# Relative-position bias factors built by matmuls from a sliding one-hot constant instead of through a DRAM buffer, in a fused attention and MLP kernel

## The chip, the cores and the metric

One core of one Trainium2 chip runs the whole program. The metric is device time in microseconds (us) of one execution, the median over several timed runs.

## The reference

Attention with a bucketed relative-position bias, then a two-layer MLP with a sine gate. B = 8 sequences, H = 8 heads, S = 576 positions, D = 64.

```python
scores = scale * np.matmul(q, k.transpose(0, 1, 3, 2))      # [8, 8, 576, 576]
rel = pos[:, None] - pos[None, :]
bucket = ...                                                # of |rel|: 0..31, 31 from |rel| near 128 on
scores = scores + bias_table[bucket].transpose(2, 0, 1)[None]
attn = softmax(scores)
x = np.matmul(attn, v)  ->  [4608, 512]
h = x @ w_in                                                # [4608, 2048]
s = np.sin(alpha * h)
g = h + s * s / (alpha + 1e-09)
out = g @ w_out                                             # [4608, 512]
```

The bias depends on a head and on the distance alone, and every distance from about 128 on shares bucket 31. So exp(score + bias) is exp(score) times a factor in a band around the diagonal, once the last bucket's value is subtracted; outside the band the factor is 1.

## The kernel before

**Tiling.** Scores are computed transposed (128 keys on the partitions, 512 queries along the row) for two heads at a time (a "pair", p = 0 to 3). A unit of kind "A" is one block of 128 keys for a pair: two matmuls of 64 rows, then one exp on ACT of 128x1024 (`ex` in `plan_unit`, L723), then on DVE the multiplication of the columns near the diagonal by the band factors (`bd`, L754). Kind "C" is the 64 keys left over, for which a pair shares one block-diagonal key tile `kts`; its band multiplication is on POOL or DVE (L740, factors `mhr`). "B" and "X" are the 64 queries left over. `plan_av` then multiplies with the values `vs`/`vhs` on PE, `norm_av` divides by the row sums on DVE (L967, L968), and for batch t = 0 PE transposes the result and ACT or DVE copies it into `xT` (L560, L562).

**Batches.** The loop over t = 0 to 7 does one sequence's attention, then a block of 512 tokens of the MLP: `plan_moe_in` (h on PE, sine on ACT at L1083, square on ACT at L1090 or DVE at L1092, g on DVE at L1097) and `plan_mo` (g times w_out on PE). The matmuls of `plan_mo` fill the next batch's attention on PE. The exps and the sines use two activation tables, so ACT loads a table twice per batch (L1161). All exps of a batch come before its first sine.

**What sets the order.** Every instruction belongs to a `Task` with an estimated cost per engine, dependencies, a priority and an earliest time (`nb`). `Plan.run` walks a modelled clock and issues tasks, which fixes the order on each engine; the engines then run in that order and wait where data is missing. `HEAD_PRI` overrides the priorities of numbered tasks. Where PE would stand idle early on, the planner inserts matmuls of zeros (`zz`) into a free bank.

**The head.** For t = 0, q and k are loaded in natural layout: pair 0 into `natx` by SP and ACT, pairs 1 to 3 into `nat1` by POOL; PE transposes them (L573, L579; `plan_tr`), DVE copies them to `kT`/`qT` (L562), POOL copies the block-diagonal `kt` (L602). For t = 1 they are loaded into `nat2` by POOL and transposed likewise; from t = 2 on they go through DRAM buffers `staged_k`/`staged_q` and DMA transposes. The values of t = 0 are loaded in float32 into the space of `w_out16` and cast by POOL (L441, L444). w_in, `nat2`, w_out and the values of t = 1 follow on POOL's queue.

**The band factors.** `plan_table` multiplies the table `tabN` by a constant that subtracts the last row (`less_last`), takes the exp on ACT (`tabE`), and multiplies by a one-hot constant `phi_sb` (32x512), which gives one row of 512 distances for each head. ACT copies the row to `e_sb` (L625), a DMA writes it five times to a DRAM buffer `e_dram`, and five DMAs on SP's queue read it back with a stride of one element per partition, which slides the row along the partitions: three into `m2r` (heads 0-1, 2-3, 4-7), two into `mhr`. The factors lie reversed there and are read backwards (`m2 = m2r[:, :, ::-1]`).

```python
load_m2r(nc.sync, 0, 2, 0)
load_mhr(nc.sync)
load_m2r(nc.sync, 2, 4, 3)
load_m2r(nc.sync, 4, H, 4)
for h in range(2, H):
    load_v32(h)
```

Of the kernel before, what the change touches and what calls it, by code (L numbers as in the profile page):

```python
# [34 lines left out]
LAT = {"PE": 0.2, "ACT": 0.18, "DVE": 0.18, "POOL": 0.2, "SP": 2.4}  # L35
NBUF = {"ut": 2, "u": 2, "g": 2, "s16": 3, "sq": 3, "outs": 5, "xn": 6}
PAIRS = ((0, 1), (2, 3), (4, 5))
BANKS = {"h": (0, 1, 2, 3, 4, 5), "av": (6, 7), "mo": (7, 6)}

# [21 lines left out]
class Plan:  # L61
# [86 lines left out]
    def run(self, t0):  # L148
        free = dict(t0)
        todo = list(self.tasks)  # L150
        while todo:
# [21 lines left out]
            for e, c in cands.items():  # L173
                if not c:
                    continue
                s0 = min(x[0] for x in c)
                st, t = min(((x[0], x[1]) for x in c if x[0] <= s0 + SLACK[e]),
                            key=lambda x: (x[1].pri, x[0]))
                fin = st + t.engs[e]
                if best is None or (st, fin) < best[:2]:  # L180
                    best = (st, fin, e, t)
# [32 lines left out]
T_START = {"PE": 4.25, "ACT": 5.2, "DVE": 5.05, "POOL": 5.5, "SP": 5.0}  # L214
SPLIT = {0: 3, 1: 3}
PRI_S = 0
T_WI = 16.4
T_TAB = 4.9
T_PHI = 5.4
T_CL = 9.6  # L220
T_FIRST = (4.3, 5.35)
T_PAIR = ((7.05, 8.1), (8.9, 10.6), (12.5, 13.4))
PRI_TR = (350, 950, 1250)
T_VT = 9.7
T_ACT = ()
T_M2 = (12.4, 14.6, 16.0, 16.0)
T_MH = 13.5
T_RST = 20.0
T_WL = 25.0
T_V0 = (6.5, 8.8, 16.4, 16.9, 17.4, 17.9, 18.4, 18.9)  # L230
T_P3 = 8.3
# [5 lines left out]
T_LD = 33.0  # L237
# [4 lines left out]
SQ = {"ACT": 0.52, "DVE": 0.38}  # L242
T_V = ((15.0, 15.0), (53.5, 53.5))
T_TR1 = (35.5, 39.0)
T_W = (24.2, 27.0, 33.0, 33.0)
T_WO = (42.0, 45.0, 47.8, 51.0)
WARM0 = 7
WARM1 = 0
# [18 lines left out]
}  # L267
SIN_SET = "trig_and_small"
SLACK = {"PE": 0.02, "ACT": 0.02, "DVE": 0.02, "POOL": 0.02, "SP": 0.02}
# [14 lines left out]
def kernel(  # L284
# [26 lines left out]
    NE = 5  # L311
# [14 lines left out]
    last_np = np.eye(NB, dtype=np.float32)  # L326
    last_np[NB - 1] -= 1.0
    phi_h = nc.inline_tensor(phi_np, "phi_const")
    last_h = nc.inline_tensor(last_np, "last_const")
# [8 lines left out]
    m2r = sgl.tile([128, H, XW], F16, name="m2r")  # L338
    mhr = sgl.tile([128, NP, 192], F16, name="mhr")
    m2 = m2r[:, :, ::-1]  # L340
    mh = mhr[:, :, ::-1]
# [13 lines left out]
    tabE = sgl.tile([NB, H], F16, name="tabE")  # L355
    phi_sb = sgl.tile([NB, EW], F16, name="phi_sb")
    less_last = sgl.tile([NB, NB], F32, name="less_last")
    e_sb = sgl.tile([H, EW], F16, name="e_sb")
    alphaN = sgl.tile([NF, 128], F32, name="alphaN")
    idf_sb = sgl.tile([NF, NF], F32, name="idf_sb")  # L360
# [43 lines left out]

    def stage_kq(t):
        for dst, src in ((staged_k, k), (staged_q, q)):
            nc.gpsimd.dma_start(
                out=dst.ap()[t].rearrange("s (h d) -> s h d", h=H),
                in_=src[t].rearrange("h s d -> s h d"),
            )  # L410

    def load_kqT(t):
        nc.sync.dma_start_transpose(out=kTs[t % 2][:, :, :], in_=staged_k.ap()[t])
        nc.sync.dma_start_transpose(out=qTs[t % 2][:, :, :], in_=staged_q.ap()[t])

    def load_kt(t):
        for z in range(2):
            r = slice(64 * z, 64 * z + 64)
            nc.gpsimd.tensor_copy(out=kts[t % 2][r, :, r], in_=kTs[t % 2][r, :, 512:S])  # L419

    def load_v16(t):
        vp = v[t].rearrange("h s d -> s h d")
        for c in range(4):
            nc.gpsimd.dma_start(  # L424
                out=vs[t % 2][:, c, :, 0:D], in_=vp[128 * c : 128 * c + 128],
            )
# [3 lines left out]
    def load_v32(h):  # L430
        nc.sync.dma_start(out=vst[:, h], in_=v[0, h, 0:512].rearrange("(c p) d -> p c d", p=128))
# [29 lines left out]
    def load_w_out16():  # L461
        src = moe_w_out.rearrange("(f p) n -> p f n", p=128)
        for fh in range(4):
            nc.gpsimd.dma_start(
# [782 lines left out]
```

## Time and profile before

| | |
|---|---|
| timed runs | 373.47, 374.05, 375.78 us, median 374.05 us |
| span of the profiled execution, first to last instruction | 372.5 us |
| the profiled execution's own time | the page gives its span alone; the timed runs lie 1.0 to 3.3 us above it, their median 1.55 us |
| PE busy | 363.7 us (98% of the span) |
| ACT busy | 318.3 us (85%) |
| DVE busy | 258.8 us (69%) |
| POOL busy | 89.2 us (24%) |
| the chain that ended last | 87% on PE; the rest, almost all of it, in its first 52.4 us |

The page names engines PE (matmul), PEld (weight load), DVE, ACT, POOL and SP; a q behind a name is the engine's queue of DMA issues. A row of the timeline gives the start, the duration, the engine, the line, the operation and its tiles, and in brackets how long the engine stood idle before it and for whom. A row by windows gives the length of the window, then the busy time of PE, PEld, DVE, ACT and POOL, then PE's granted clock (1.00 is full), the DMA engines' share and their rate. A busy PE is modelled, and matmuls overlap, so PE's rows read a little too full.

### The profile page before, as it was taken

The page shows a single profiled execution, that of the slowest core. Times are in us where ns is not written, and L with a number is a line of the kernel's source. Part 1 is how long each engine was busy: PE and PEld are TensorE (multiplying, and loading weights), DVE is VectorE, ACT ScalarE, POOL GpSimd, SP SyncE. Part 2 cuts the span into 40 slices and gives each one's busy share as a digit, 9 for nine tenths or more (in the row PEclk, how much of TensorE's full clock was granted, in tenths as well). Part 3 has the DMA queues.
Part 4 walks back from the last instruction along what each step waited for, and adds up shares of the span by engine and source line. Part 5 has one row for each costly group of instructions (what it writes and reads, how often), then busy time and mean ns, then how long its engine had stood idle before and what let it go on. Part 6 is the DMA issues. An engine that isn't in the chain of part 4 may idle for free.

```text
span 372.5 us, 8907 instructions
## 1 busy us (share of the span) xinstructions
PE 363.7 (98%) x3563; PEld 195.3 (52%) x3563; DVE 258.8 (69%) x555; ACT 318.3 (85%) x436; POOL 89.2 (24%) x130
## 2 busy tenths in 40 slices
PE   6989989999999999999999999999999999999996
PEld 2455445644465445784554456444676455444443
DVE  4697966678776967597659866787669675879100
ACT  2898999989998999799989999899979997999211
POOL 5575360065000730064003700090006000000000
PEclk9599999999999999999999999999999999999999
DMA  9799999299824996199917992699249121000122
GB/s 167 152 191 208 203 170 155 61 146 123 113 60 99 115 151 112 48 161 138 135 48 135 126 169 59 115 114 171 60 111 118 65 58 48 7 18 13 59 85 84
DMA packets 149690, 40.69 MB, mean 109 GB/s; under 512 B 137144, under 2 KB 144656, under 8 KB 149648
## 3 DMA queue, kind: packets, MB, share of 16 engines
q0 software_dynamic: 94928, 17.47, 58.1%
q1 hardware_dynamic: 54352, 22.30, 25.5%
q8 instruction: 28, 0.46, 0.5%
q10 hardware_dynamic: 368, 0.34, 0.3%
q14 instruction: 14, 0.11, 0.1%
HBM read 37.73 MB, written 16.56 MB: 146 GB/s over the span
## 4 chain that ended last, share of the span: by engine, by line
PE 87%; DVE 4%; DMA 3%; ACT 3%; issue 1%; SPq 0%; ACTq 0%; DVEq 0%
PE pb L478 86%; DVE g L1097 1%; DMA tabN<-in_bias_table_dram 1%; DVE u L754 1%; DMA m2r<-e_dram 1%; DMA e_dram<-e_sb 1%; ACT sq L1090 1%; PE pb L1039 1%; ACT s L1083 1%; ACT nat L723 1%; DVE sq L1092 0%; DVE kT L562 0%; ACT L1161 0%; SPq L501 0%; DVE xn L968 0%
## 5 line engine op out<-in xcount | busy, mean ns | idle before, releaser
L723 ACT ACTIVATE u<-pb 128x1024 f16<-128x1024 f32 (+1 forms) x146 | 137.6, 1015 | 8.8 <-PE pb L478 7.4
L478 PE MATMUL pb<-w_out,g 128*128 128x512 f16 (+2 forms) x592 | 138.7, 374 | 0.5 <-DVE kT L562 0.5
L478 PE MATMUL pb<-xT,w_in 128*128 128x512 f16 (+4 forms) x704 | 127.5, 340 | 0.0
L1097 DVE SCALAR_TENSOR_TENSOR g<-sq,inv_a,pb 128x512 f16<-128x512 f16 x144 | 101.1, 743 | 7.7 <-ACT sq L1090 3.8
L1083 ACT ACTIVATE s<-pb,alphaT 128x512 f16<-128x512 f32 x144 | 92.9, 692 | 11.1 <-PE pb L478 10.2
L478 PEld LDWEIGHTS <-w_in 128*128 128x128 f16 x704 | 64.6, 98 | 57.1
L754 DVE TENSOR_TENSOR u<-u,m2r 128x768 f16<-128x768 f16 (+1 forms) x128 | 63.2, 498 | 35.6 <-ACT u L723 33.7
L478 PEld LDWEIGHTS <-g 128*128 128x128 f16 x592 | 54.0, 98 | 60.3 <-issue 5.4
L478 PEld LDWEIGHTS <-u 128*128 128x128 f16 x1152 | 43.1, 97 | 10.9 <-issue 5.8
L1090 ACT ACTIVATE sq<-s 128x512 f16<-128x512 f16 x75 | 46.8, 637 | 1.2 <-DVE g L1097 0.3
L419 POOL COPY kt<-kT 64x256 f16<-64x256 f16 x12 | 5.1, 428 | 174.2 <-DMA kT<-staged_k 144.9
L478 PE MATMUL pb<-qT,kT 64*128 64x64 f16 (+1 forms) x512 | 44.0, 293 | 1.6 <-ACT u L723 0.6
L478 PE MATMUL pb<-v,u 128*128 128x65 f16 x1024 | 43.7, 193 | 0.0
L1092 DVE TENSOR_TENSOR sq<-s 128x512 f16<-128x512 f16 x69 | 28.8, 427 | 12.1 <-ACT s L1083 11.2
L968 DVE TENSOR_TENSOR xn<-pb,rd 128x256 f16<-128x256 f32 (+2 forms) x59 | 28.5, 483 | 2.0
L478 PEld LDWEIGHTS <-kT 64*128 64x128 f16 x512 | 16.3, 95 | 23.1 <-issue 16.2
L478 PE MATMUL pb<-vh,u 128*128 128x130 f16 x128 | 28.3, 221 | 0.0
L424 POOL DMA_DIRECT2D v<-in_v_dram x28 | 24.8, 898 | 6.9 <-DMA w_in<-in_moe_w_in_dram 2.6
L560 ACT ACTIVATE outs<-pb 128x512 f32<-128x512 f32 (+2 forms) x10 | 5.5, 554 | 19.9 <-PE pb L478 19.9
L562 DVE COPY outs<-pb 128x512 f32<-128x512 f32 x27 | 18.5, 686 | 3.8 <-PE pb L478 3.8
L1161 ACT ACT_TABLE_LOAD x15 | 19.2, 1283 | 0.3
L967 DVE RECIPROCAL rd<-pb 128x4 f32<-128x4 f32 (+2 forms) x59 | 11.0, 186 | 10.8 <-PE pb L478 10.7
(74 smaller groups left out, 181.2 us busy)
## 6 DMA issues: line engine op xcount, KB each, us to landing
out_dram<-outs SPq DMA_DIRECT2D x35, 256.0 KB, 2.3
v<-in_v_dram POOLq DMA_DIRECT2D x28, 128.0 KB, 5.1
staged_k<-in_k_dram POOLq DMA_DIRECT2D x6, 576.0 KB, 9.6
staged_q<-in_q_dram POOLq DMA_DIRECT2D x6, 576.0 KB, 12.0
w_out<-in_moe_w_out_dram POOLq DMA_DIRECT2D x4, 512.0 KB, 17.4
w_out<-in_v_dram SPq DMA_DIRECT2D x8, 128.0 KB, 5.2
w_in<-in_moe_w_in_dram POOLq DMA_DIRECT2D x2, 512.0 KB, 6.3
w_in<-in_moe_w_in_dram POOLq DMA_DIRECT2D x1, 1024.0 KB, 11.6
```

The source lines that it names most:

```text
L424: nc.gpsimd.dma_start(out=vs[t % 2][:, c, :, 0:D], in_=vp[128 * c : 128 * c + 128],)
L478: nc.tensor.matmul(out=out, lhsT=lhsT, rhs=rhs, start=start, stop=stop)
L562: k_of(e).tensor_copy(out=o, in_=i)
L723: nc.scalar.activation(out=o, in_=x, func=AF.Exp, scale=0.125)
L754: nc.vector.tensor_tensor(out=io, in0=io, in1=m2[:, 2 * p : 2 * p + 2, x0 : x0 + hi - lo], op=ALU.mult)
L967: nc.vector.reciprocal(out=r, in_=x[:, :, :, D])
L968: nc.vector.tensor_tensor(out=xn[:, 0:n].rearrange("p c (z d) -> p c z d", z=2), in0=x[:, :, :, 0:D], in1=r.unsqueeze(3).to_broadcast([128 ...
L1083: nc.scalar.activation(out=s16.v, in_=h.v, func=AF.Sin, scale=alphaT[:, f : f + 1])
L1090: nc.scalar.activation(out=sq.v, in_=s16.v, func=AF.Square)
L1092: k_of(e).tensor_tensor(out=sq.v, in0=s16.v, in1=s16.v, op=ALU.mult)
L1097: nc.vector.scalar_tensor_tensor(out=gcell[b].v[:, f, :], in0=sq.v, scalar=inv_a[:, f : f + 1], in1=h.v, op0=ALU.mult, op1=ALU.add,)
L1161: nc.scalar.preload_act_table_set(name)
```

## The change

- **Band factors on PE.** The one-hot constant becomes 128x512: four copies of the 32 buckets, each shifted by one distance, and in its last four columns a mark for each copy. The table's exp now has 128 rows (four copies); DVE multiplies it by the marks into `tab4` (128 rows, 8 heads x 4). A matmul with 128 neighbouring columns of the constant as weights and `tab4` as the moving operand (32 columns) gives four columns of the band for all heads at once, already slid along the partitions. 96 such matmuls, in three groups of 32, make a 128x8x384 band in three PSUM pairs; ACT copies two of them into `m2` and DVE the third (1024 float32 columns each). `mh` is copied from `m2`, one half by DVE and one by POOL. The DRAM buffer, its write and the five reads, and `e_sb`, are gone; the factors are read forwards.
- **Table first.** `tabN` is loaded as the first DMA on POOL's queue; it was the fourth on ACT's. `less_last` is made on DVE from the identity instead of loaded. The constant (now 128 KB, it was 32 KB) is the third DMA on ACT's queue; it was the third on SP's.
- **First values by chunks of keys.** Four loads of 256 KB each for 128 keys of all heads, all issued at the start on SP's queue; before, eight of 128 KB, one for each head, two at the start and six behind the band reads. The eight casts on POOL, one for each head, now need all four.
- **Order.** The third pair load follows the second at once on POOL. w_in is issued on POOL right behind them, before any value is cast. w_out, the values of t = 1 and the staging of t = 2 follow as transfers with their own modelled queue. Most earliest times are replaced by dependencies on modelled transfers, the remaining ones have new numbers, and `HEAD_PRI` lists a priority for every early task.

ACT from the cast of the first q on (natx: the first pair; pb: PSUM; the tile that `order` prints as m is `m2`; `u` rows are exps). Before:

```order
L540 ACTIVATE natx<-natx 96x6x64
L616 ACTIVATE tabE<-pb 32x8
L625 ACTIVATE e_sb<-pb 8x512
L626 DMA e_dram<-e_sb 8x5x512
L723 ACTIVATE u<-pb 128x2x512 x3
L723 ACTIVATE u<-pb 128x512
L723 ACTIVATE u<-pb 128x2x512 x2
```

Now:

```order
L561 ACTIVATE natx<-natx 96x6x64
L633 ACTIVATE tabE<-pb 128x8
L577 ACTIVATE m_76<-pb 128x8x128
L795 ACTIVATE u<-pb 128x2x512 x3
L795 ACTIVATE u<-pb 128x512
L577 ACTIVATE m_76<-pb 128x8x128
L795 ACTIVATE u<-pb 128x2x512 x5
```

One copy of a third of the band stands ahead of the first exp and another behind the fourth; the copy of `e_sb` and the DMA issue are gone.

DVE from the copy of alpha on to the first multiplications by the band (CAST of m is the copy of the band's last third out of PSUM). Before:

```order
L665 COPY alphaT<-pb 128x16
L666 TENSOR_SCALAR tmp_a<-alphaT 128x16
L669 RECIPROCAL inv_a<-tmp_a 128x16
L562 COPY qT_68<-pb 128x576
L754 TENSOR_TENSOR u<-u,m2r 128x2x384
L754 TENSOR_TENSOR u<-u,m2r 128x2x256
L562 COPY kT_66<-pb 128x576
```

Now:

```order
L734 COPY alphaT<-pb 128x16
L737 TENSOR_SCALAR tmp_a<-alphaT 128x16
L740 RECIPROCAL inv_a<-tmp_a 128x16
L579 COPY qT_68<-pb 128x576
L666 COPY mh<-m_76 64x768
L579 CAST m_76<-pb 128x8x128
L579 COPY kT_66<-pb 128x576
L827 TENSOR_TENSOR u<-u,m_76 128x2x256
L827 TENSOR_TENSOR u<-u,m_76 128x2x384 x2
```

Two copies, one half of `mh` and a third of the band, now stand between the copy of pair 2's q and the first multiplication, and pair 3's k is copied before it too. Further up, the product `tab4` now stands between the first copies of k and q.

POOL behind the first pair loads (nat is `nat1`, kt the block-diagonal keys, v and vh the values). Before:

```order
L531 CAST idf_sb<-id_sb 16x16
L602 COPY kt_70<-kT_66 64x64 x2
L454 DMA nat_96<-in_k_dram 96x2x384
L454 DMA nat_96<-in_q_dram 96x2x384
L602 COPY kt_70<-kT_66 64x64 x2
L441 CAST vh_74<-w_out_79 64x4x64 x2
L602 COPY kt_70<-kT_66 64x64 x2
L444 CAST v_72<-w_out_79 128x4x64 x2
```

Now:

```order
L487 DMA nat_96<-in_k_dram 96x2x384
L487 DMA nat_96<-in_q_dram 96x2x384
L619 COPY kt_70<-kT_66 64x64 x2
L492 DMA w_in_78<-in_moe_w_in_dram 128x4x512 x2
L492 DMA w_in_78<-in_moe_w_in_dram 128x4x1024
L619 COPY kt_70<-kT_66 64x64 x2
```

The last pair load now precedes the first copy to `kt`, and the loads of w_in follow that copy; before, they stood among the casts of values. Behind these rows come memsets, two casts of values, the `kt` copy of pair 2, a third cast and one half of `mh`, the other six casts of values later. The table's load and the identity's cast stand ahead of all pair loads.

On PE the first group of 32 band matmuls stands ahead of the first scores; then come two A units, both transposes of pair 1, an A and a C unit, the first transpose of pair 2, the second group, an A unit, the second transpose of pair 2, and the third group. Before, the scores followed the 32x512 product at once, and one transpose stood behind each of the first three units.

The diff, cut to its core:

```diff
+LAT = {..., "DMA": 1.9}
-T_WI = 16.4
+T_WI = 8.0
-T_FIRST = (4.3, 5.35)
+T_FIRST = (4.75, 5.65)
-T_V0 = (6.5, 8.8, 16.4, 16.9, 17.4, 17.9, 18.4, 18.9)
+T_V0 = (12.3,) * 8
 HEAD_PRI = {
-    0: 3652.1, 1: 2400.7, 3: 2400.3, ...
+    0: 9015.789063, 1: 9014.578049, 2: 9014.559597, ...
...
-    e_dram = nc.dram_tensor("e_dram", [NE, 4 * H, EW], F16, kind="Internal")
-    phi_np = np.zeros((NB, EW), dtype=np.float16)
-    for x in range(EW - 1):
-        phi_np[bt[abs(x - 255)], x] = 1.0
+    phi_np = np.zeros((NJ * NB, EW), dtype=np.float16)          # NJ = 4
+    for j in range(NJ):
+        for x in range(EW - NJ):
+            phi_np[NB * j + bt[abs(x - 252 - j)], x] = 1.0
+        phi_np[NB * j : NB * j + NB, EW - NJ + j] = 1.0
...
+    P_.dma_start(out=tabN, in_=bias_table)
...
-    nc.scalar.dma_start(out=less_last, in_=last_h.ap())
-    nc.scalar.dma_start(out=tabN, in_=bias_table)
-    nc.sync.dma_start(out=phi_sb, in_=phi_h.ap())
+    nc.scalar.dma_start(out=phi_sb, in_=phi_h.ap())
...
-    load_v32(0)
-    load_v32(1)
+    for c in range(4):
+        load_v32(c)
...
+    load_pair(3)
...
+    nc.vector.tensor_scalar(out=less_last, in0=idf_sb..., scalar1=idf_sb[:, NB - 1 : NB], op0=ALU.subtract)
...
+        def spread(e):
+            nc.vector.tensor_tensor(
+                out=tab4, in0=tabE.unsqueeze(2).to_broadcast([NJ * NB, H, NJ]),
+                in1=phi_sb[:, EW - NJ : EW].unsqueeze(1).to_broadcast([NJ * NB, H, NJ]), op=ALU.mult,
+            )
...
+        for k, w in enumerate((1, 2, 0)):
+            def mm(e, b=b, w=w, s=0):
+                o = bank(b, 2).rearrange("p k x -> p (k x)")
+                for i in range(n // NJ // 2 * s, n // NJ // 2 * (s + 1)):
+                    x0 = EW - NJ - 128 - n * w - NJ * i
+                    full(o[:, NJ * H * i : NJ * H * (i + 1)], phi_sb[:, x0 : x0 + 128],
+                         tab4.rearrange("p h j -> p (h j)"), True, True)
+            def cp(e, b=b, w=w):
+                copy_on(e, m2[:, :, n * w : n * (w + 1)]..., bank(b, 2)...)
+        for z in range(2):
+            def half(e, z=z):
+                k_of(e).tensor_copy(out=mh[r], in_=m2[r, z::2, 64 * z : 64 * z + 192])
...
-        for h in range(2, H):
-            load_v32(h)
...
-        x = plan.add({"POOL": 1.7}, lambda e: load_nat2(), [], 9021, nb=T_RST, after=[x])
-        x = plan.add({"POOL": 3.2}, lambda e: load_w_out16(), [], 9022, nb=T_WL, after=[x] + vdone)
+    def plan_loads():
+        ...                        # w_in, nat2, w_out, values of t = 1, staging of t = 2,
+        ...                        # each a POOL issue and a transfer on a modelled DMA queue
```

More of the change, by code (lines that the diff above doesn't have):

```diff
@@ L34 @@
 D_TAIL = 0.72
-LAT = {"PE": 0.2, "ACT": 0.18, "DVE": 0.18, "POOL": 0.2, "SP": 2.4}
+LAT = {"PE": 0.2, "ACT": 0.18, "DVE": 0.18, "POOL": 0.2, "SP": 2.4, "DMA": 1.9}
 NBUF = {"ut": 2, "u": 2, "g": 2, "s16": 3, "sq": 3, "outs": 5, "xn": 6}
@@ L241 @@
 NORM0 = 1200
[L242 to L246, printed above, removed]
+SQ = {"ACT": 0.53, "DVE": 0.41}
 WARM0 = 7
+COLD = (99.0, 99.0, 1.0)
 WARM1 = 0
@@ L310 @@
     EW = 512
-    NE = 5
+    NJ = 4
     ctx.enter_context(tc.manual_schedule())
@@ L512 @@
     )
+    P_.tensor_copy(out=idf_sb, in_=id_sb[0:NB, 0:NB])
     for kq, src in ((0, k), (1, q)):
@@ L608, in plan_table @@
     def plan_table():
-        a, b = Buf("h"), Buf("h")
+        a = Buf("h")
         def less(e):
-            full(bank(a)[0:NB, 0:H], less_last, tabN, True, True)
+            full(bank(a)[:, 0:H], less_last.rearrange("a j b -> a (j b)"), tabN, True, True)
         def ex(e):
-            nc.scalar.activation(out=tabE, in_=bank(a)[0:NB, 0:H], func=AF.Exp)
-        x = plan.add({"PE": 0.15}, less, [], -1200, nb=T_TAB, new=[a])
-        x = plan.add({"ACT": 0.15}, ex, [x], -1200, use=[a])
-        def mm(e):
-            full(bank(b)[0:H, 0:EW], tabE, phi_sb, True, True)
@@ L742, in bd @@
                 )
-            d = plan.add({"POOL": 0.6} if t == 0 and p else {"DVE": 0.25 if two else 0.15}, bd, [x],
-                         base + 10, nb=late, use=[ub])
+            d = plan.add({"POOL": 0.6} if t == 0 and p else {"DVE": 0.25 if two else 0.15}, bd, [x] + band,
+                         base + 10, use=[ub])
             for pp in (p, p + 1) if two else (p,):
```

256 lines of the change are left out of this document (151 added, 105 removed), and 39 rows, old and new, of the table HEAD_PRI.

## The prediction

> **What bounds the kernel now.** I read the page's totals first, then the busy time by windows, then the chain of waits, then the groups of single windows.
>
> ```profile
> PE 363.7 (98%) x3563; PEld 195.3 (52%) x3563; DVE 258.8 (69%) x555; ACT 318.3 (85%) x436; POOL 89.2 (24%) x130
> ...
> 4.82:8.23 3.41, 1.47 (x22) 1.01 (x21) 1.34 (x3) 0.73 (x3) 1.66 (x4) 1.00 1.19 173
> 8.23:11.65 3.42, 3.42 (x38) 1.68 (x38) 1.65 (x3) 2.60 (x3) 0.71 (x3) 0.50 1.13 189
> 11.65:15.06 3.41, 3.41 (x35) 1.58 (x33) 2.05 (x6) 3.21 (x4) 2.30 (x8) 0.50 0.35 71
> 15.06:18.46 3.40, 3.40 (x35) 1.52 (x33) 2.89 (x6) 2.88 (x5) 1.93 (x9) 0.50 0.92 214
> 18.46:29.67 11.21, 10.02 (x177) 6.95 (x176) 10.95 (x30) 10.59 (x16) 8.74 (x16) 1.00 1.16 197
> 29.67:52.40 22.73, 21.40 (x220) 10.39 (x217) 17.26 (x32) 21.67 (x36) 11.35 (x19) 1.00 1.39 199
> 52.40:369.70 317.30, 317.20 (x3046) 171.11 (x3045) 220.66 (x471) 275.07 (x373) 58.66 (x65) 1.00 0.80 97
> ```
>
> From 52.40 to 369.70 PE stands idle for 0.10 us (317.30 - 317.20). The change adds and removes nothing there, so those 317 us stay. Whatever it does must show before 52.4 us: as an earlier start of PE's unbroken work (29.67, the first matmul with w_in) or as less PE idle between 29.67 and 52.40, which is 22.73 - 21.40 = 1.33 us.
>
> ```profile
> 2.22 4.77 DMA tabN<-in_bias_table_dram
> ...
> 8.19 0.59 ACT e_sb L625
> 8.81 3.42 DMA e_dram<-e_sb
> ...
> 13.96 4.43 DMA m2r<-e_dram
> 18.48 1.61 DVE u L754 x3
> ```
>
> The chain runs through the DRAM bounce: from the table's load at 2.22 to the first multiplication by the last heads' factors at 18.48. Read alone, it promises ten microseconds. But a chain names only the wait that ended last. Beside it stands ACT:
>
> ```profile
> 9.39 2.18 ACT L723 ACTIVATE u<-pb 128x1024 f16<-128x1024 f32 x2 [0.61 <-PE pb L478]
> ...
> 26.30 2.43 ACT L723 ACTIVATE u<-pb 128x1024 f16<-128x1024 f32 x3 [0.59 <-PE pb L478]
> ...
> L723 ACT ACTIVATE u<-pb 128x1024 f16<-128x1024 f32 x16 | 15.8, 1026 | 1.5 <-PE pb L478 1.4
> L723 ACT ACTIVATE u<-pb 128x512 f16<-128x512 f32 x4 | 2.4, 600 | 0.6 <-PE pb L478 0.5
> ```
>
> The 20 exps of t = 0 run from 9.39 to 28.73 (26.30 + 2.43), 19.34 us, and do not need the factors at all. The idle before them is 1.5 + 0.6 = 2.1, of which 0.61 lies before 9.39; so 1.5 us of the 19.34 are gaps and 17.85 are work. No sine may come before the last exp. DVE is the second wall: 10.95 of the 11.21 us from 18.46 on are busy, because its multiplications began late.
>
> **The change, part by part.** *When the first exp starts.*
>
> ```profile
> 7.12 0.20 PE L478 MATMUL pb<-tabN,less_last 32*32 32x8 f32 x2 [1.94 <-DMA tabN<-in_bias_table_dram]
> ...
> 5.04 0.52 ACT L540 ACTIVATE natx<-natx 96x384 f16<-96x384 f32 x1 [1.07 <-DMA natx<-in_q_dram]
> 5.17 0.76 DVE L562 COPY kT<-pb 128x576 f16<-128x576 f16 x1
> ...
> 8.74 0.61 PE L478 MATMUL pb<-qT,kT 64*128 64x512 f16 x2
> ```
>
> PE stood 1.94 us for the table, and the transposes of q stood behind it. As the first DMA on POOL the table's issue moves from 2.22 to 0.81. I take its landing as before 5.5, since a landing at 0.81 + 4.77 = 5.58 is the same duration without the queue ahead of it. ACT's cast of q ends at 5.56, so the table's exp ends near 5.9. DVE's copy of k ends at 5.93; the product `tab4` follows when the constant has landed. It stands behind the first q on ACT's queue, which landed at 5.04; with four times the bytes I take 6.3. Then `tab4` is there at 6.5, the first band group runs from 6.7 to 7.6, the first scores until 7.85 and ACT's first band copy until 8.7 to 9.0. The first exp starts at 9.0, against 9.39: -0.4 us, although the table is 2 us earlier.
>
> *The 96 band matmuls.* No row shows 32 columns on 128 weight columns. The nearest:
>
> ```profile
> 48.43 0.64 PE L478 MATMUL pb<-qT,kT 64*128 64x64 f16 x32
> 41.95 0.45 PE L579 MATMUL pb<-id_sb,nat 96*64 96x96 f16 x12
> 19.18 0.41 PE L478 MATMUL pb<-v,u 128*128 128x65 f16 x8
> ...
> 9.28 0.69 PE L579 MATMUL pb<-id_sb,nat 96*64 96x96 f16 x12
> ```
>
> Per instruction these rows give 20, 38 and 51 ns at full clock, so a group of 32 lies between 0.64 and 1.6 us; part of each row is the pipeline's fill, which a group pays once, and I take 0.9. At the half clock the third row becomes the fourth (0.45 to 0.69 us), so I take up to 2.1 there. Groups two and three hide behind exps that are already queued, if PE is at full clock.
>
> *Copies out of PSUM.*
>
> ```profile
> 52.50 6.70 ACT L723 ACTIVATE u<-pb 128x1024 f16<-128x1024 f32 x7
> ```
>
> One 128x1024 exp takes 1.03 us in its row and 0.95 from start to start ((6.70 - 1.03) / 6 in this run of seven), and a band copy on ACT has the same size: two of them. The first precedes the first exp and is in the 9.0; the second adds **0.95**. ACT's 0.59 for `e_sb` fell before 9.39 and frees nothing later. DVE's third copy is priced by a line through two rows of the profile:
>
> ```profile
> L562 DVE COPY outs<-pb 128x512 f32<-128x512 f32 x27 | 18.5, 686 | 3.8 <-PE pb L478 3.8
> ...
> L562 DVE COPY kT<-pb 128x576 f16<-128x576 f16 x6 | 4.5, 756 | 2.2 <-PE pb L579 2.1
> ...
> L754 DVE TENSOR_TENSOR u<-u,m2r 128x768 f16<-128x768 f16 x8 | 4.3, 552 | 0.0
> ...
> L754 DVE TENSOR_TENSOR u<-u,m2r 128x512 f16<-128x512 f16 x8 | 4.5, 568 | 0.2 <-DMA m2r<-e_dram 0.2
> ```
>
> The first of these is the page's, the second the first 60 us's, the last two those of 15.4 to 30.8. Per column the first two give 1.3 ns, so 1024 columns cost 1.1 to 1.4 us; with 0.4 for a half of `mh`, DVE has 1.6 us more ahead of its first multiplication. Its idle time before 18.46 covers that (3.41 - 2.05 and 3.42 - 1.65 in two windows). The multiplications start near 15.5 to 16, as they do now, but none of the later ones waits for a DMA, and the 256-column form, 568 ns on average, has stalls in it that no busy engine explains (the larger form takes 552). I let DVE end up to 1.2 us earlier than now; ACT then decides.
>
> *Sum for t = 0.* First exp 9.0, work 17.85, second copy 0.95, gaps 0.4 instead of 1.5: last exp at 28.2, against 28.73. That is 0.5 earlier; with DVE's earlier end on the tail behind it I take **-0.6** for PE's unbroken start.
>
> *The MLP block of t = 0 and the start of t = 1.* The order gives ACT 8 squares and 3 copies of t = 1's keys and queries before the next exps, where it now has 10 and 4:
>
> ```profile
> L1090 ACT ACTIVATE sq<-s 128x512 f16<-128x512 f16 x10 | 6.6, 657 | 0.0
> L560 ACT ACTIVATE kT<-pb 128x576 f16<-128x576 f16 x2 | 1.4, 682 | 0.0
> L560 ACT ACTIVATE qT<-pb 128x576 f16<-128x576 f16 x2 | 1.3, 672 | 0.0
> ```
>
> That is 2 x 0.66 + 0.68 = 2.0 us less on ACT, which was full there (21.67 of 22.73), and 3 transposes instead of 0 come behind the first matmuls of `plan_mo`. DVE gets the two squares and stays near 16 us. So PE waits less for ACT and DVE; it can win at most its 1.33 us of idle, and I take **-1.0**. The earlier w_in, `nat2` and w_out gain nothing: no wait of PE before 52.4 is for them.
>
> *Total:* -0.6 - 1.0 = -1.6. Against the execution shown, 372.5 becomes 370.9; the span lies 1.55 below the median of the runs, and the median 374.05 becomes **372.4**. Bounds: a first exp at 8.6, no gap, DVE's tail and all of the 1.33 won give -3.5; nothing won and the losses below give up to +2.
>
> **The rivals.** *All of it is won.* If the constant lands by 5.9, ACT has no gaps and DVE no stalls, the start of PE's work moves by 2.0 and 1.3 more are won: **370.7**. For it: ACT's gaps are all waits for PE, which stood at half clock. Against: every estimate must fall right.
>
> *The bias was hidden anyway.* ACT gets two copies more and the first exp starts where it did; the gains of order are eaten: **374.0**. For it: the exps never waited for a factor.
>
> *The half clock stays (the slower case).* The granted clock is 0.50 from 8.23 to 18.46, after a window with PE busy 1.47 of 3.41 us; the three windows at half clock are each full by the modelled rows. In the changed order PE has about 1.47 + 0.9 = 2.4 us to do in 4.82 to 8.23, still not full. If the clock halves, groups two and three take 2.1 us instead of 0.9; each stands ahead of scores for which ACT waits, so the last exp comes 2 x 1.2 = 2.4 later: -0.6 + 2.4 - 1.0 = +0.8, **374.9**. It turns the sign from 0.8 us more for a group on (2 x 0.8 = 1.6). The Trainium skill's page "TensorE: Matmul & The Clock Gate", Part 1, has the clock return after one busy window of about 3.4 us, and Part 4 says that transposes do not count as busy in the same way. The spacing of 3.41 us agrees with this trace; a return after one full window does not, since it took three, and Part 4's many transposes would explain that. By Part 1's rule the clock would be back at 11.65 and only one group slow, at most 373.7; by the three windows of this trace both are, 374.9.
>
> *Values crowd out keys.* Four value loads of 256 KB now compete with the pair loads from the start.
>
> ```profile
> q0 software_dynamic: 458, 0.32, 111.4%
> ...
> q1 hardware_dynamic: 1327, 0.33, 83.5%
> q0 software_dynamic: 184, 0.13, 45.1%
> ```
>
> These are the DMA queues in 6 to 8 us and in 8 to 10: beside SP's values, POOL's queue fell from 0.32 to 0.13 MB in 2 us. Pairs 1 and 2 are 0.59 MB; at that rate from 5 on they land near 14, where PE, by my walk along its changed order, wants the last of them by about 11 to 12.5. Two to three microseconds late at the transposes, and half of `mh` on POOL waits for the values too: -0.6 + 2.6 - 0.5 = +1.5, **375.5**, with a tail to 378. Against: the eight value loads of before, two early, were only a third of it, but POOL's queue still won most of the time. [...]
>
> **How the numbers follow.** Forecast 372.4 (371.3 to 373.3): 0.40. All won, 370.7 (369.3 to 371.3): 0.25. Hidden, 374.0: 0.14. Half clock, 374.9: 0.13. Crowding, 375.5 and more: 0.08. About 1%, 3.7 us, is what a measurement of this kernel can tell from no change: below 370.3 lies a bit over half of the second case, 0.15; above 377.8 half of the last, 0.04, and 0.01 for what I have not seen; the rest, 0.80, is the same. The range, 369.8 to 375.4, leaves out a third of the second case and most of the last.
>
> **What the new profile would show.** Right: the first exp near 9.0, the last near 28.2, the first w_in matmul near 29.1, PE idle of some 0.3 between there and the unbroken stretch, and 317 us after it. The clock between 8.2 and 15 settles the third rival; PE's waits for `nat` the fourth; DVE's first band multiplication shows whether 15.5 to 16 holds. Wrong would be a gap of several microseconds on ACT between exps, a PE wait for the constant or the table, or anything different after 52 us.

## The result: 2.7% slower

The changed kernel takes 384.81 us (median of 4 runs, 383.84 to 386.48), the kernel before 374.91 us beside it on the same chip (373.47 to 376.73). The ratio is 1.0273, with a 95% interval of 1.0223 to 1.0323. The forecast was 372.4, with a range of 369.8 to 375.4: wrong in its sign, by 12 us. Ratios and intervals are those of the record, worked out over the single runs; they are not quite the quotients of the medians.

### The profile after

The profiled execution took 384.57 us with a span of 382.5. These are its windows, in the columns shown before (window, its length, PE, PEld, DVE, ACT, POOL busy with counts, granted clock, DMA share, GB/s):

```profile
17.00:20.36 3.36, 1.57 (x9) 0.60 (x8) 0.68 (x2) 3.36 (x5) 0.00 (x0) 1.00 1.22 206
20.36:34.00 13.64, 4.22 (x40) 2.52 (x41) 5.05 (x10) 2.62 (x4) 8.85 (x19) 0.50 0.42 74
40.08:62.66 22.58, 22.58 (x219) 10.40 (x216) 18.79 (x35) 21.16 (x35) 9.50 (x15) 1.00 1.53 155
40.08:378.91 338.83, 338.83 (x3266) 181.79 (x3262) 240.85 (x509) 291.89 (x400) 66.31 (x79) 1.00 0.81 99
```

The same view of the kernel before, from its first w_in matmul to PE's last one:

```profile
29.67:369.61 339.94, 338.60 (x3266) 181.51 (x3262) 237.92 (x502) 296.73 (x407) 70.01 (x83) 1.00 0.84 104
```

PE's first matmul with w_in moves from 29.67 to 40.08, 10.4 us later. Behind it are the same 3266 matmuls as before, without a gap: 338.83 us instead of 339.94. So the loss lies ahead of 40.08, but for 0.7 us at the end: the span goes on for 3.6 us behind PE's last matmul (382.5 - 378.91) where it was 2.9 (372.5 - 369.61). The windows show where: from 20.36 to 34.00 PE is busy for 4.22 of 13.64 us.

The timeline of the changed kernel, all engines, shortened to the rows that carry the first 30 us (start, duration, engine, line, operation; in brackets the idle time before it and what ended it):

```profile
7.00 1.06 PE L510 MATMUL pb<-tab,phi_sb 128*128 128x32 f16 x32
...
7.07 1.51 POOL L492 DMA_DIRECT2D w_in<-in_moe_w_in_dram  x2
...
9.06 3.35 ACT L795 ACTIVATE u<-pb 128x1024 f16<-128x1024 f32 x4
...
14.07 1.21 DVE L579 CAST m<-pb 128x1024 f16<-128x1024 f32 x1
...
15.91 1.77 DVE L827 TENSOR_TENSOR u<-u,m 128x512 f16<-128x512 f16 x4
...
24.66 0.75 POOL L477 CAST v<-w_out 128x256 f16<-128x256 f32 x2 [11.64 <-DMA w_out<-in_v_dram]
...
25.93 0.61 PE L510 MATMUL pb<-qT,kt 128*128 128x256 f16 x2 [6.68 <-POOL kt L619]
26.57 1.51 ACT L795 ACTIVATE u<-pb 128x512 f16<-128x512 f32 x2 [6.13 <-PE pb L510]
27.27 0.23 DVE L813 TENSOR_TENSOR u<-u,mh 128x128 f16<-128x128 f16 x1 [9.58 <-POOL mh L666]
...
29.59 0.27 PE L510 MATMUL pb<-vh,u 128*128 128x130 f16 x1 [3.05 <-POOL vh L474]
```

Up to 17 us nearly everything is as forecast. Then GpSimd stands 11.64 us for the values, and behind that cast in its queue stand the key copy of pair 2 (PE waits 6.68), its half of `mh` (DVE waits 9.58) and the tail rows (PE waits 3.05). ACT stands because PE does. The chain of waits begins with the values:

```profile
4.00 1.22 SPq L462
...
5.27 19.28 DMA w_out<-in_v_dram
...
24.66 0.75 POOL v L477 x2
```

The value load (`vst` lies in w_out's tile, hence its name here) was issued by 5.22 and landed at 24.55. Why it took 19 us is in the DMA queues. These are q1 (SyncE, the values) in 4 to 6 us, and then both queues in 14 to 16 and in 20 to 22; q0 is GpSimd's queue, with w_in behind the pair loads (packets, MB, busy share of the engines):

```profile
q1 hardware_dynamic: 1349, 0.34, 98.9%
...
q0 software_dynamic: 309, 0.30, 89.3%
q1 hardware_dynamic: 307, 0.08, 29.8%
...
q0 software_dynamic: 173, 0.35, 92.2%
q1 hardware_dynamic: 175, 0.04, 17.2%
```

With GpSimd's queue still almost empty (21 packets), the values move at 0.34 MB in 2 us. In 10 to 12 us that queue carries the pair loads: 395 packets of some 0.7 KB to 397 of the values, which go down to 0.10 MB in 2 us. That is not yet w_in; the run with w_in behind the fourth cast, below, has 398 to 396 there. Soon after 12 us w_in follows. The queues go on packet for packet, 309 to 307 and 173 to 175; but a packet of the values is 256 bytes (1.18 MB in 4608 packets), one of w_in about 1 KB (0.30 MB / 309) and in its last load 2 KB (0.35 MB / 173). What is left of the 1.18 MB of values (four loads of 256 KB, two of 64), 0.45 MB at 12 us, goes down to 0.08 and then 0.04 MB in 2 us. In the kernel before, w_in was issued from 20.68 on, and in 18 to 20 us q1 stood alone:

```profile
q1 hardware_dynamic: 1778, 0.57, 123.1%
```

The theory for the experiments: not the bands, the table or the copies, but the w_in loads, moved from 20.7 to 7.1 us, starve the value loads, and GpSimd's in-order queue passes the wait on. The rivals: the chunked form of the value loads is at fault whatever runs beside it; GpSimd's queue is at fault and not the values; the DMA engines are short of bandwidth, whatever the size of the packets.

### The profile page after: what moved, and what is told of

It reads as the page before. It is cut to its first block, busy times and chain, and to the rows that moved or that the text cites. A ratio compares the mean times of both kernels' runs of the same rounds, so it can differ in the third digit from the quotient of the medians.

```text
span 382.5 us, 9081 instructions
## 1 busy us (share of the span) xinstructions
PE 366.0 (96%) x3662; PEld 199.9 (52%) x3662; DVE 263.0 (69%) x566; ACT 314.4 (82%) x430; POOL 91.0 (24%) x132
## 4 chain that ended last, share of the span: by engine, by line
PE 90%; DMA 6%; POOL 1%; ACT 1%; SPq 0%; issue 0%; POOLq 0%; ACTq 0%
PE pb L510 89%; DMA w_out<-in_v_dram 5%; ACT u L795 1%; DMA natx<-in_k_dram 1%; PE pb L596 1%; POOL v L477 1%; PE pb L1113 0%; SPq L462 0%; POOL vh L474 0%; POOL kt L619 0%; POOL mh L666 0%; ACT outs L577 0%; ACT xT L577 0%; PE pb L1023 0%; POOLq L477 0%
## 5 line engine op out<-in xcount | busy, mean ns | idle before, releaser
L827 DVE TENSOR_TENSOR u<-u,m 128x512 f16<-128x512 f16 (+1 forms) x128 | 62.5, 496 | 32.3 <-ACT u L795 30.2
L510 PEld LDWEIGHTS <-u 128*128 128x128 f16 x1152 | 44.7, 98 | 14.2 <-issue 6.2
L510 PE MATMUL pb<-v,u 128*128 128x65 f16 x1024 | 44.8, 195 | 1.0 <-POOL v L477 0.8
L510 PE MATMUL pb<-qT,kT 64*128 64x64 f16 (+1 forms) x512 | 42.5, 289 | 0.7 <-ACT u L795 0.6
```

The costliest lines, as they stand in the source:

```text
L510: nc.tensor.matmul(out=out, lhsT=lhsT, rhs=rhs, start=start, stop=stop)
L827: nc.vector.tensor_tensor(out=io, in0=io, in1=m2[:, 2 * p : 2 * p + 2, x0 : x0 + hi - lo], op=ALU.mult)
```

## The experiments

"PE's start" is the first w_in matmul. Each ratio is to the kernel before on the same chip, which took 374.14 to 375.82 us beside the experiments; go by the ratios and not by differences of the medians.

| kernel | median us | ratio (95% interval) | PE's start |
|---|---|---|---|
| before | 374.91 | | 29.67 |
| changed | 384.81 | 1.0273 (1.0223 to 1.0323) | 40.08 |
| w_in behind the fourth cast | 379.61 | 1.0100 (1.0079 to 1.0121) | 33.13 |
| values by heads 0 to 7, w_in early | 385.25 | 1.0249 (1.0227 to 1.0271) | 41.47 |
| casts held back, w_in early | 382.60 | 1.0192 (1.0160 to 1.0224) | 38.08 |
| kernel before, w_in early | 382.28 | 1.0177 (1.0153 to 1.0201) | 37.51 |
| w_in behind the memsets | 376.31 | 1.0026 (1.0003 to 1.0048) | 32.00 |
| the same, tail rows first | 376.21 | 1.0044 (1.0020 to 1.0067) | 31.68 |
| values in 1 KB packets, w_in early | 374.16 | 0.9989 (0.9956 to 1.0022) | 29.52 |
| tail rows first, heads in cast order | 374.43 | 0.9978 (0.9949 to 1.0007) | 31.16 |
| the same, more fill matmuls | 373.44 | 0.9979 (0.9955 to 1.0003) | 29.55 |
| heads in cast order, w_in early | 380.66 | 1.0163 (1.0118 to 1.0208) | 36.42 |

### w_in behind the fourth cast

```
-  pool("w%d" % i, ..., lambda x0=x0, x1=x1: load_w_in16(x0, x1), ...)
+  pool("w%d" % i, ..., lambda x0=x0, x1=x1: w_late.append((x0, x1)), ...)
   def cast_then(h):            # in place of cast_v(h) in plan_v0
       cast_v(h)
+      if fourth cast: for x in w_late: load_w_in16(*x)
```

> The changed kernel with one thing moved back: the three w_in loads are issued on GpSimd behind the fourth cast of values instead of ahead of the key copy of pair 1. Band, table, order of everything else as in the changed kernel. Theory A (w_in's packets take turns with the values' 256-byte packets, one for one, and hold them back): without w_in in the queues the values land near 13.5 to 14 us instead of 24.55, GpSimd's casts of values do not wait until 24.66, the multiplications that started at 15.91 go on, the last exp ends near 28.2 and PE's unbroken start is near 30; time 370.5 to 372.5, so faster than the changed kernel by some 13 us. Theory B (the casts wait for all four chunks, and four loads of 256 KB behind each other are late whatever runs beside them): values land after 20 us also here, the stall stays, time 380 to 385.

GpSimd's and PE's timeline of this kernel:

```profile
14.68 0.75 POOL L477 CAST v<-w_out 128x256 f16<-128x256 f32 x2 [2.39 <-DMA w_out<-in_v_dram]
...
18.81 2.25 POOL L492 DMA_DIRECT2D w_in<-in_moe_w_in_dram  x3
21.04 1.17 POOL L474 CAST vh<-w_out 64x256 f16<-64x256 f32 x2
...
22.26 0.27 PE L510 MATMUL pb<-vh,u 128*128 128x130 f16 x1 [2.78 <-POOL vh L474]
...
40.84 0.38 PE L510 MATMUL pb<-w_out,g 128*128 128x512 f16 x1 [1.28 <-DMA w_out<-in_moe_w_out_dram]
```

The first cast goes at 14.68 instead of 24.66: theory A's mechanism, and B falls. The time did not follow all the way, 379.61 where 370.5 to 372.5 was expected. The edit itself put 2.25 us of issues ahead of the tail rows' casts, for which PE waited until 22.26, and it sent w_out late. So this run shows when the values land, but not yet what the rest of the change is worth.

### Values by heads, w_in early

```
-  out=vst[:, :, c], in_=v[0, :, 128 * c : 128 * c + 128].rearrange("h p d -> p h d")   # 4 loads
+  out=vst[:, h], in_=v[0, h, 0:512].rearrange("(c p) d -> p c d", p=128)               # 8 loads, 0 to 7
```

> The changed kernel with w_in still issued early, but the values loaded by heads (eight loads of 128 KB: heads 0 and 1, the tail rows, then heads 2 to 7) instead of by four chunks of keys of all heads, so that a cast waits for its own head alone. Theory A (turn-taking of packets): the queue's total stays as slow and the last head lands near 24, but heads 0 to 3 land by about 11; GpSimd's first casts do not stall, and what is behind them in its queue goes on; most of the loss is gone, casts of heads 6 and 7 (20 to 24 us) may still cost something; time 371 to 375. Theory B (w_in early costs its ten microseconds whatever the form of the value loads, because DMA throughput is short until 24 us): time 381 to 385.

SyncE's and GpSimd's timeline:

```profile
5.60 12.14 SPq L462 DMA_DIRECT2D w_out<-in_v_dram  x6
...
12.06 0.40 POOL L475 CAST v<-w_out 128x256 f16<-128x256 f32 x1
24.88 0.41 POOL L475 CAST v<-w_out 128x256 f16<-128x256 f32 x1 [12.42 <-DMA w_out<-in_v_dram]
```

385.25: theory A's time was missed by ten microseconds. The order written for GpSimd casts heads 1, 5, 7, 2, 3, 0, 4, 6. Head 1 was there by 12.06, but the second cast wants head 5, one of the last loaded. So this run tells nothing against the turns; it was the wrong order of heads. The last six issues alone hold SyncE for 12.14 us.

### Casts held back, w_in early

```
   def cast_then(h):            # in place of cast_v(h) in plan_v0
+      held.append(h)           # casts 1 to 3 are emitted with the fourth,
+                               # behind the key copies of pairs 2, 3 and the half of mh
```

> The changed kernel, w_in early and values by chunks, but the first three casts of values held back on GpSimd and done together with the fourth, behind the key copies of pairs 2 and 3 and GpSimd's half of mh. This splits the stall: what stood behind the casts in GpSimd's queue against what needs the values themselves. Theory A1 (the queue is most of it): keys' copies and mh come at 13 to 16 us, scores, exps and multiplications go on to near 28, only the matmuls with the values wait for 24.6 us and come in a heap behind it; PE's unbroken start near 32, time 375 to 378. Theory A2 (the values are all of it, the matmuls with them hold PE's in-order queue and the PSUM buffers of the scores as long): PE's start near 39 to 40 as now, time 383 to 385.

GpSimd's and PE's timeline:

```profile
23.78 1.44 POOL L477 CAST v<-w_out 128x256 f16<-128x256 f32 x4 [5.91 <-issue]
...
27.28 0.27 PE L510 MATMUL pb<-vh,u 128*128 128x130 f16 x1 [7.63 <-POOL vh L474]
```

The key copies and `mh` are free, and still PE waits 7.63 us for the tail rows. 382.60 lies between the two, nearer A2: the queue behind the first casts is worth some 2 to 3 of the 10 us lost (PE's start comes 2.0 earlier, the ratio falls from 1.0273 to 1.0192), the late values the rest.

### The kernel before, w_in early

```
   load_pair(3)
+  for x0, x1 in ((0, 1), (1, 2), (2, 4)):
+      load_w_in16(x0, x1)      # from 8.11 instead of 20.68
```

> The kernel before the change, with its three w_in loads issued behind the keys and queries of pair 3 (near 8 us) instead of at 20.7 to 23.9; nothing else changed. Theory A (turn-taking): the reads of the bounced factors and the value loads, which stand on the other queue, share turns with w_in's packets; the last heads' m2r lands near 21 to 22 instead of 18.4 and the values later still; PE's unbroken start 2 to 8 us later, time 376 to 382. Theory B (w_in's early issue is harmless by itself, and only the chunked order of the value loads made the loss): time 373.5 to 375, as before.

DVE's and PE's timeline, and then the queues in 18 to 20 us, where q1 stood alone before with 1778 packets:

```profile
22.18 0.90 DVE L759 TENSOR_TENSOR u<-u,m2r 128x768 f16<-128x768 f16 x2 [6.61 <-DMA m2r<-e_dram]
...
37.51 0.81 PE L478 MATMUL pb<-xT,w_in 128*128 128x512 f16 x3
```

```profile
q0 software_dynamic: 168, 0.33, 88.4%
q1 hardware_dynamic: 154, 0.12, 23.6%
```

382.28 us, 1.0177 (1.0153 to 1.0201): moving w_in alone, with no bands, no chunks and no new order, costs about two thirds of what the whole change costs. B falls. The victims are other transfers: the write of `e_dram` takes 5.75 us (8.72 to 14.47) instead of 3.42, then come the reads into `m2r`, then the values. Turns nearly one for one (154 to 168) show only from 18 us on. The write sent 22 and 25 packets in the two stretches of 2 us from 10 on, beside 330 and 334 of GpSimd's queue, and the reads, issued from 14.49 on, have no packet before 18 (before the change they were issued from 12.24 on and had packets by 14). What held these two is not shown, so this run shows the price of the early w_in and only in part how it comes about.

### w_in behind the memsets, and the tail rows first

```
   def clear_then(e):           # in place of clear(P_, 1)
       clear(P_, 1)
+      cast_vt()                # second run only, with load_vt32() ahead of the chunks
+      for x in w_late: load_w_in16(*x)
```

> The changed kernel with the three w_in issues put on GpSimd behind the seven memsets (near 12.2 us), directly ahead of the first cast of values. In the run with w_in behind the fourth cast, values landed at 14.57, but the issues (2.25 us) then stood ahead of the casts of the tail rows, the first matmul with values came at 22.26, and w_out, last in GpSimd's queue of transfers, came 1.28 us late for its matmul at 40.84. Theory (what was left there is GpSimd's own order): now the issues fall into GpSimd's wait, w_in's packets meet only the last of the values' packets, which land near 15.5 to 17; the first matmul with values comes near 20.5 to 21.5 and the wait for w_out goes; time 376 to 378. Rival (any w_in packet ahead of the values' end costs as much as in the changed kernel): 381 to 385.

> As the run with w_in behind the memsets, and the 64 tail rows of values are loaded ahead of the four chunks on SyncE and cast on GpSimd ahead of the w_in issues, instead of last of the loads and behind the fourth cast. Theory (the in-order queue of GpSimd holds the first matmul with values; it needs the tail rows and two heads): the tail rows are ready near 13, the first matmul with values comes near 19.5 to 20.5, the last exp near 29, PE's unbroken start near 30; time 372.5 to 375.5. Rival (the tail rows were not what was late; the chunks and the casts behind each other are): no gain over that run, 376 to 378.

GpSimd's and PE's timeline of the first of the two:

```profile
11.93 2.25 POOL L492 DMA_DIRECT2D w_in<-in_moe_w_in_dram  x3
15.15 0.75 POOL L477 CAST v<-w_out 128x256 f16<-128x256 f32 x2 [0.98 <-issue]
...
21.41 0.60 PE L510 MATMUL pb<-v,u 128*128 128x65 f16 x8 [0.86 <-POOL v L477]
```

376.31 in the first: three issues moved by 5 us on one queue, 7.07 to 11.93, take back 8.1 of the 10.4 us at PE's start (40.08 to 32.00), and the ratio falls from 1.0273 to 1.0026. Their 2.25 us lie in GpSimd's wait. The tail rows first gain nothing (376.21), as the rival said: PE waits for a head's cast instead (1.10 us at 21.70 in the second).

### Values in 1 KB packets, w_in early

```
-  out=vst[:, :, c], in_=v[0, :, 128 * c : 128 * c + 128].rearrange("h p d -> p h d")
+  out=vst[:, 2 * c : 2 * c + 2],
+  in_=v[0, 2 * c : 2 * c + 2, 0:512].rearrange("h (p c) d -> p h c d", c=4)
```

> The changed kernel with w_in early, as it is, but each of the four value loads takes two heads with four neighbouring rows to a partition: packets of 1 KB instead of 256 bytes, 1152 packets instead of 4608, the same bytes. The rows of the values stand in another order then, so the output differs; nothing else changes. Theory (turns are per packet, so a queue of small packets starves beside one of large packets): the values land before 11 us, GpSimd does not wait, the first matmul with values comes near 19.5, PE's unbroken start near 29.5; time 371 to 374. Rival (the DMA engines are simply short of bandwidth until 24 us, whatever the packets): the values land after 18 us, time 379 to 385.

GpSimd's and PE's timeline, and both queues in 10 to 12 us:

```profile
11.99 0.75 POOL L478 CAST v<-w_out 128x256 f16<-128x256 f32 x2
...
29.52 0.81 PE L511 MATMUL pb<-xT,w_in 128*128 128x512 f16 x3
```

```profile
q0 software_dynamic: 374, 0.26, 84.6%
q1 hardware_dynamic: 367, 0.16, 41.3%
```

This is the run that decides against a bandwidth that is short whatever the packets. The bytes, the queues and the early w_in are those of the changed kernel, and the turns are again one for one (374 to 367, here of the values with the pair loads); but the first cast goes at 11.99 and GpSimd never waits for the values. PE starts at 29.52 instead of 40.08, and the time is 374.16, 0.2 above the range expected. The 10 us are a matter of the size of the packets: with 1 KB the four value loads are through before w_in's first packets come, near 12 us, so this run does not show w_in beside packets of 1 KB. The two queues also moved more in all, 1.42 MB in 6 to 12 us instead of 1.20, and how much of the gain is share and how much is total was not separated. A load now brings two whole heads instead of 128 keys of all; the runs with loads by heads and an early w_in, at 385.25 and 380.66, show that this alone does not take the loss away. The kernel leaves out putting the rows back in their order, so it is a test and not a version to use.

### Heads in cast order: w_in behind the memsets, and early

```
-  for c in range(4): load_v32(c)
+  for h in (1, 5, 7, 2, 3, 0, 4, 6): load_v32(h)     # behind the tail rows
```

> As the run with w_in behind the memsets and the tail rows first, and the values loaded by heads, in the order in which GpSimd casts them (1, 5, 7, 2, 3, 0, 4, 6). In the first run by heads they were loaded 0 to 7, and the second cast, of head 5, waited until 24.88. Theory: heads 1 and 5 land by 11, no cast waits for more than a microsecond, the first matmul with values comes near 19 to 19.5, PE's unbroken start near 29 to 29.5, and what was forecast of the change comes out: 371.5 to 374. Rival (loads by heads are no better than by chunks once w_in is out of the way): as the run with the tail rows first, 372.5 to 375.5.

> The run with values by heads in cast order and the tail rows first, but w_in issued early again, where the changed kernel has it (7 us). It ends the square of two choices: values by chunks or heads, w_in early or behind the memsets. Theory (turns are per packet, and a cast needs its own head alone): the queue's end stays late, the last heads land near 22 to 25, but heads 1, 5, 7 and 2 land before 14; the casts of the last two heads hold up the half multiplications and the later transfers on GpSimd; some 2 to 5 us are lost against w_in behind the memsets, 375.5 to 379. Rival (w_in early costs as in the changed kernel whatever the order of the heads): 382 to 385.

With w_in behind the memsets, 374.43: a cast no longer waits for the values, and the ratio, 0.9978, lies clear below the 1.0044 of loads by chunks with the tail rows first. But the time is 0.4 above the theory's range, and PE's start is 31.16 and not 29 to 29.5. The windows show why:

```profile
16.26:19.67 3.41, 2.31 (x14) 1.06 (x13) 2.69 (x6) 3.41 (x5) 3.11 (x7) 1.00 1.23 202
19.67:23.08 3.41, 2.37 (x29) 1.71 (x28) 3.38 (x8) 2.23 (x4) 3.41 (x6) 0.50 1.19 213
23.08:26.50 3.42, 3.42 (x37) 2.25 (x35) 2.01 (x7) 1.56 (x2) 2.51 (x5) 0.50 1.13 206
```

PE had been waiting for ACT and GpSimd, its clock was granted at 0.50 from 19.67 to 26.50, and ACT, busy 1.56 of 3.42 us at the end, then waited for PE. With w_in early the same loads give 380.66, between theory and rival. GpSimd's timeline there:

```profile
19.93 0.46 POOL L475 CAST v<-w_out 128x256 f16<-128x256 f32 x1 [2.02 <-DMA w_out<-in_v_dram]
25.51 0.40 POOL L475 CAST v<-w_out 128x256 f16<-128x256 f32 x1 [5.12 <-DMA w_out<-in_v_dram]
```

Five heads are there by 20 us, the sixth at 25.5. A good order of heads saves some 4 us; it does not stand in for keeping w_in off.

### More fill matmuls

```
   def warm1(k, n):
-      full(pb[:, k, 0:n], zz[:, 0:128], zz[:, 0:n], True, True)
+      for _ in range(3 if n == 192 else 1):
+          full(pb[:, k, 0:n], zz[:, 0:128], zz[:, 0:n], True, True)
```

> The run with values by heads in cast order and w_in behind the memsets, and each of PE's five fill matmuls of 192 columns (between 13.8 and 21.7 us) is made three times instead of once. There PE's clock was granted at 0.50 from 19.67 to 26.50, behind a stretch of 3.41 us in which PE was busy for 2.31 us; in the runs so far stretches up to 2.31 were followed by the half clock and those from 2.38 on were not. Theory (the half clock is what is left of the loss: PE's unbroken start at 31.16 where 29.1 was forecast): some 0.5 us more of busy time holds the clock at 1.00, the last exp ends near 28.5 and PE's unbroken start is near 29.3 to 29.8; 372 to 373.5. Rival (GpSimd's queue of casts, which made PE wait until 20.71, sets that start whatever the clock): PE's start near 31 and 374 to 375, as before.

PE's windows, and then ACT's last exp and PE's start in the timeline:

```profile
8.76:12.17 3.41, 2.60 (x57) 1.76 (x57) 2.54 (x6) 3.41 (x5) 2.38 (x10) 1.00 1.23 200
12.17:15.58 3.41, 3.41 (x59) 2.07 (x59) 2.23 (x4) 2.82 (x4) 3.31 (x7) 0.50 0.93 169
15.58:18.99 3.41, 3.10 (x38) 1.50 (x35) 3.11 (x6) 3.30 (x5) 3.06 (x8) 1.00 1.24 206
18.99:22.40 3.41, 2.88 (x39) 1.86 (x38) 3.41 (x7) 3.41 (x5) 3.41 (x7) 1.00 1.17 202
```

```profile
27.30 1.06 ACT L803 ACTIVATE u<-pb 128x1024 f16<-128x1024 f32 x1
...
29.55 0.81 PE L508 MATMUL pb<-xT,w_in 128*128 128x512 f16 x3
```

From 15.58 on the clock is full, the last exp ends at 28.36, and PE starts at 29.55 instead of 31.16, as the theory has it. The median falls from 374.43 to 373.44, but the two ratios (0.9978 and 0.9979) can't be told apart. The spans of the single runs say more: without the added fill 6 of 10 took 372.4 to 374.1 us, all six with a mean clock of 0.991 (6.8 us at half clock), and 4 took 371.3 to 371.9; with it 1 of 12 took 373.6, again at 0.991, and 11 took 371.1 to 371.9. So the fill makes the costly half clock rare; the two kernels ran on different chips, which this leaves open. The version is no slower than the kernel before; that it is faster is not shown (the interval reaches to 1.0003).

## Why the prediction was wrong

**The step that failed** is one sentence in the part on the MLP block: "The earlier w_in, `nat2` and w_out gain nothing: no wait of PE before 52.4 is for them." That PE never waited for them is true. But the step only asked who wants these transfers, and not beside whom they now run. Moved from 20.7 to 7.1 us, 2 MB in packets of 1 and 2 KB stood from 12 us on beside the last 0.45 MB of values in packets of 256 bytes, which GpSimd did want: they landed at 24.55, and at 14.57 in the run with w_in behind the fourth cast. Its term in the sum was 0; at PE's start it measured about +8 to +10. Three runs give it: with w_in behind the memsets and nothing else moved, the changed kernel gains 8.1 us at PE's start (40.08 to 32.00); with large value packets it gains 10.6 (40.08 to 29.52); and the kernel before with w_in early loses 7.8 (29.67 to 37.51).

**The rival "values crowd out keys"** saw that the two queues would slow each other, and still missed: it priced SyncE's values as the aggressor and the pair loads as the victim, at 1.5 us with a tail to 378. The trace shows the reverse. With turns one for one, the queue with the smaller packets loses, and that was the values' (0.10 MB against 0.28 beside the pair loads, 0.04 against 0.35 beside w_in). Its rows were misread too: they do not show that the values made GpSimd's queue fall from 0.32 to 0.13 MB. By 8 us pairs 1 and 2 had moved 0.54 of their 0.59 MB and pair 3 had only been issued from 6.44 on, and 1327 packets to 184 are no turns one for one. It had noted that half of `mh` on GpSimd waits for the values, but had not followed what else stands behind that cast.

**What held.** The first exp was to start at 9.0 and did at 9.06; a band group was to take 0.9 us and took 1.06 and twice 0.97; DVE's third copy was to take 1.1 to 1.4 and took 1.21; the multiplications were to start at 15.5 to 16 and did at 15.91. The -1.0 for PE's idle behind its first w_in matmul came as -1.1 (339.94 to 338.83): the stretch of 22.58 us that answers to 29.67 to 52.40 has no gap. It is not an effect of the late start: with PE's start at 29.52 (1 KB packets) and 29.55 (more fill) the same matmuls take 339.04 and 338.96. The reason held as well: ACT does 8 squares and 3 copies there, where it did 10 and 4. DVE did not stay near 16 us of that stretch, it takes 18.79, but PE does not wait for it. So of the parts that the forecast worked out step by step most came out within a few tenths of a microsecond, and a term set to nothing was larger than all of them together.

**What fell short.** The -0.6 for PE's start. In the best run the last exp ends at 28.36 (28.2 forecast), but PE starts at 29.55, 0.1 earlier than before and not 0.6: what DVE and PE do behind the last exp took 1.2 us there (29.55 - 28.36) where before it took 0.9 (29.67 - 28.73). That run, the change with four edits on top (w_in later, tail rows first, heads in cast order, more fill), comes to -1.1 us by the profiled spans (372.5 to 371.4), where -1.6 was forecast for the change alone. And one bound of the forecast does not close: -3.5 from 374.05 gives 370.55, but the case that wins all was let down to 369.3 without a term for it.

**The half clock.** It did not come at the place of the rival: in the changed kernel the clock is full until 20.36. In the run with 1 KB packets it did come there, and a band group took 1.03 us, little more than the 0.97 at full clock and far from the 2.1 of the rival:

```profile
10.89:14.30 3.41, 3.41 (x87) 2.66 (x82) 1.99 (x5) 2.54 (x4) 2.99 (x11) 0.50 1.27 199
...
11.41 1.03 PE L511 MATMUL pb<-tab,phi_sb 128*128 128x32 f16 x32
```

In the changed kernel the half clock came as a second cost wherever PE had to wait, from 20.36 to 34.00, and from 19.67 to 26.50 in the run with heads in cast order, about 1.6 us there by the start of PE (31.16 against 29.55).

## What to carry to other kernels

When a change moves a load earlier, ask not only who waits for it but which loads will be in flight beside it, and compare packets and not bytes: two queues took turns one packet each, so the load with 256-byte rows moved a quarter to a ninth of w_in's bytes. A load that nobody wants for 20 us should be issued behind the one that is wanted next; where it stands in its queue can be worth more than the whole change around it. And a cast that waits for a load, on an in-order engine, is a gate for everything behind it: list that too.

## What the runs showed of the hardware

**Two DMA queues that both have packets waiting take turns packet by packet.** 395 to 397, 309 to 307, 173 to 175 and 374 to 367 in 2 us each, over sizes from 256 bytes to 2 KB. The Trainium skill's page "DMA: Bandwidth & Descriptors", section "Queues, rings and completion order", has each engine go round its queues at the granularity of packets; these counts agree. The kernel before with w_in early is the exception on record, up to 18 us.

**The clock changes at a spacing of 3.41 us, but not by a sharp number of busy time.** Where the half clock came, it stayed for one or several stretches of 3.41 us. It followed stretches with PE busy for 2.31 us (16.26 to 19.67, heads in cast order) and 2.60 (8.76 to 12.17, more fill matmuls), but not this one of the run with 1 KB packets, with 2.54:

```profile
17.72:21.13 3.41, 2.54 (x29) 1.44 (x28) 3.41 (x8) 3.41 (x6) 3.29 (x7) 1.00 1.15 214
```

So the border that I gave ahead of the last run, between 2.31 and 2.38, doesn't hold. The busy times are modelled, and the stretch with 2.60 holds 18 transposes while this one holds none; whether they count otherwise was not tried. The granted clock on record can also be missing: in the kernel before with w_in early it reads 1.00 throughout, but two matmuls of 512 columns take 0.61 us there until 32.09, as they do at 0.50, and 0.39 from 33.80 on. One full stretch brought the clock back at 15.58, where the kernel before needed three. The Trainium skill's page "TensorE: Matmul & The Clock Gate", Part 1, gives one busy window for the return: the last run agrees, the kernel before does not.
